# Larger handover and move allowances in the planner of a fused attention and MLP kernel, past the first fifth of the plan

## The chip, the cores and the metric

The kernel runs on one core of one Trainium2 chip. Such a core has five instruction streams: TensorE (PE in the profile; its weight loads are listed apart as PEld), VectorE (DVE), ScalarE (ACT), GpSimd (POOL) and SyncE (SP), which here does nothing but issue DMAs. Every stream runs its instructions strictly in the order in which the program lists them, and waits on semaphores for the others. The metric is the device time of one execution in microseconds (us), as the median of several runs.

## The reference, cut to what matters

```python
# q, k, v: 8 batches x 8 heads x 576 x 64;  f: 8 x 8 x 576
scores = (q @ k.T) / sqrt(64)
cum    = cumsum(log(clip(f, 1e-4, 1)))
scores = where(causal, -1e9, scores + cum[:, None] - cum[None, :])
attn   = exp(scores - max(scores)); attn /= sum(attn) + 1e-9
x      = attn @ v                      # as 4608 tokens x 512
h      = x @ w_in                      # 512 -> 2048
g      = h * tanh(softplus(h))         # Mish
out    = g @ w_out                     # 2048 -> 512
```

## The kernel before

Attention goes by pairs of heads, four pairs a batch, 32 in all. For each pair after the first batch PE multiplies queries by keys (tile `st`) into a PSUM bank `b`; DVE adds the mask and takes the row extreme in one pass (`b<-b,mskw`, and the small `mn`); ACT takes the exponential into one of four buffers (called `rk` or `more_e` by their memory); ACT rounds it to a high fp16 half and DVE subtracts to get the low half (both `hb`); a transposing DMA on the SP queue turns `hb` into `pt`; PE multiplies `pt` by the values `vv`. The sums are normalised (`x<-b,rr`), split into halves (`xp`) and turned by DMA into `xa`, the tokens of the MLP.

The MLP goes by nine chunks of 512 tokens. First layer: `xa` by the weights `wall` into banks b2 and b3, Mish on ACT into `me`, then a high half `gh` (on ACT or DVE) and a low half `gl` (DVE). Second layer: `gh` and `gl` by `wall` into banks b4 to b7, then `ot` and a DMA to memory. Scores use banks b0 to b3 as well while the MLP runs, so b2 and b3 are shared between scores and the first layer. The MLP of one chunk runs while the attention of the next batch is computed; the first 200 us hold the preparation of the weights and the attention of the first batch.

No order is written by hand. `Program` records every operation with its possible engines (`choose` may offer, say, `gh` to ACT or DVE), and `emit` (line 332) lists them in the order that `schedule` (line 370) finds. `schedule` alternates two passes ten times and keeps the best of the orders by its own replay `played` (line 392). `backward` (line 443) walks the plan from its end, with fixed delays from one engine to another (`DELAY`, line 368) and a fixed time for a DMA; the latest start that it finds for an operation becomes its priority. `forward` (line 483) is a list scheduler: it gives each engine the ready operation with the best priority and puts the result ready at its end, plus `DELAY`, plus an allowance from `MARGIN` (line 132), 100 ns for PE, DVE and ACT, 0 for POOL, 300 ns for a DMA. The same sum holds for when a PSUM bank may be used again. `forward` also picks the engine of an operation with several ways (`sooner`, line 506). Planned times are in ns. The order alone reaches the chip: an allowance is no wait in the program, it only makes the planner put other ready work between a producer and its consumer.

Of the kernel before, what the change touches and what calls it, by code (L numbers as in the profile page):

```python
# [129 lines left out]
LOOK = dict(zip(('tensor', 'vector', 'scalar', 'gpsimd', 'sync'), (float(x) for x in ("0", "0", "0", "0", "0",))))  # L130
PRIO = 200
MARGIN = dict(tensor=100,vector=100,scalar=100,gpsimd=0,sync=300)
DRAWS = 4
WORK, LAGS, MOVES = 0.02, 50.0, 300.0
F32COL = 8.3
# [30 lines left out]
class Program:  # L166
# [203 lines left out]
    def schedule(self, deps):  # L370
# [12 lines left out]
        for k in range(FB + 1):  # L383
            end, order, ends = self.forward(deps, succ, [a - b for a, b in zip(rank, self.leads)])
            end = float(np.mean([self.played(succ, order, x) for x in range(DRAWS)])) if DRAWS else end
            if best is None or end < best[0]:
# [56 lines left out]
    def backward(self, deps, succ, order, ends):  # L443

        ops = self.ops
        n = len(ops)
        way = dict(order)
        need = [len(x) for x in succ]
        ready = [0.0] * n
        clock = {q: 0.0 for q in self.NAMES}  # L450
        coming = {q: [] for q in self.NAMES}
        ripe = {q: [] for q in self.NAMES}
        end = max(ends)
        start = [0.0] * n
        for i in range(n):
            if not need[i]:
                heappush(coming[ops[i][0][way[i]][0]], (0.0, i))
        left = n
        while left:
            t, q = min(  # L460
                (clock[q] if ripe[q] else max(clock[q], coming[q][0][0]), q)
                for q in self.NAMES if ripe[q] or coming[q])
            while coming[q] and coming[q][0][0] <= t:
                i = heappop(coming[q])[1]
                heappush(ripe[q], (-ends[i], i))
            i = heappop(ripe[q])[1]
            cost = ops[i][0][way[i]][2]
            clock[q] = t + (max(cost) if q == "sync" else cost[0] / 2.4 + 2.5 if q == "tensor" else cost)
            start[i] = end - clock[q]
            left -= 1  # L470
            for j in deps[i]:
                p, _, c, _ = ops[j][0][way[j]]
                if p == "sync":
                    d = 1580.0 + c[0] + c[1] - max(c)
                else:
                    d = 0.0 if p == "tensor" and q == "tensor" else self.DELAY[p]
                ready[j] = max(ready[j], clock[q] + d)
                need[j] -= 1
                if not need[j]:
                    heappush(coming[p], (ready[j], j))  # L480
        return start

    def forward(self, deps, succ, rank):
# [6 lines left out]
        clock = {q: 0.0 for q in self.NAMES}  # L490
# [11 lines left out]
        def arrive(i):  # L502
            for o, (q, _, _, _) in enumerate(ops[i][0]):
                heappush(coming[q], (ready[i], i, o))
# [22 lines left out]
        while len(order) < n:  # L527
            clock["sync"] = max(clock["sync"], hw, dma - BACK)
            best = None
            for q in self.NAMES:  # L530
                r, c = ripe[q], coming[q]
                while r and taken[r[0][1]]:
                    heappop(r)
                while c and taken[c[0][1]]:
                    heappop(c)
                if r or c:
                    t = clock[q] if r else max(clock[q], c[0][0])
                    if best is None or (t, q) < best:
                        best = (t, q)
            t, q = best  # L540
            while coming[q] and coming[q][0][0] <= t:
                _, i, o = heappop(coming[q])
                if not taken[i]:
                    heappush(ripe[q], (rank[i], i, o))
            skipped, far = [], None
            other = read if q == "tensor" else written
            got = None
            while ripe[q]:
                x = heappop(ripe[q])
                if taken[x[1]]:  # L550
                    continue
                late = max([other.get(b, 0.0) for b in self.banks[x[1]]], default=0.0)
                if late > t:
                    heappush(coming[q], (late, x[1], x[2]))
                    continue
                if len(ops[x[1]][0]) > 1 and sooner(x[1], x[2], q, t):
                    skipped.append(x)
                    continue
                f = self.sets[x[1]]
                if q == "scalar" and f not in (None, table) or q == "tensor" and self.forms[x[1]] != form:  # L560

                    if far is None:
                        far = x
                    else:
                        skipped.append(x)
                    continue
                if far is not None and x[0] > far[0] + (TSWAP if q == "scalar" else 0 if form == (True, True) else MSWAP):
                    heappush(ripe[q], x)
                else:
                    got = x  # L570
                break
            if far is not None:
                if got is None:
                    got = far
                else:
                    skipped.append(far)
            for x in skipped:
                heappush(ripe[q], x)
            if got is None:
                if not ripe[q]:  # L580
                    continue

                later = [clock[p] for p in self.NAMES if p != q and ripe[p]]
                later += [max(clock[p], coming[p][0][0]) for p in self.NAMES if coming[p]]
                clock[q] = max(t + 20.0, min([v for v in later if v > t], default=t + 20.0))
                continue
            key, i, o = got
            wait = [
                (rank[k], k, ok, tk) for tk, k, ok in coming[q]
                if tk <= t + LOOK[q] and rank[k] < key and not taken[k] and len(ops[k][0]) == 1]  # L590
            if wait:
                heappush(ripe[q], got)
                _, i, o, t = min(wait)
            taken[i] = True
            order.append((i, o))
            _, way, cost, lock = ops[i][0][o]
            if way[0][1].startswith("dma_start"):
                hw = max(t, hw) + cost[0]
                clock[q] = t + 50
                dma = max(dma, hw + 650) + cost[1]  # L600
                end, own = dma + 930 + MARGIN["sync"], 0.0
            else:
                if q == "tensor":
                    cols, weight, h = cost
                    slow = 1.0 if left.get(int(t / TICK) - 1, 0.0) >= 3060.0 else 2.0
                    cost = 22.0 if h and half and h != half else cols * slow / 2.4 + (2.5 if slow < 2 else 0.0)
                    a, b = (t + 197.0) / TICK, (t + 197.0 + cols * slow / 2.4) / TICK
                    for k in range(int(a), int(b) + 1):
                        left[k] = left.get(k, 0.0) + weight * (min(b, k + 1) - max(a, k)) / (b - a)
                    half = h  # L610
                    if self.forms[i] != form:
                        form = self.forms[i]
                        cost += MSW * slow
                elif lock:
                    port = max(t, port) + cost
                    cost = port - t
                elif q == "scalar" and self.sets[i] not in (None, table):
                    table = self.sets[i]
                    cost += 1370.0
                clock[q] = t + cost  # L620
                end, own = clock[q], self.DELAY[q] + MARGIN[q]
            ends[i] = end
            for b in self.banks[i]:
                (written if q == "tensor" else read)[b] = end + own
            for j in succ[i]:
                d = 0.0 if q == "tensor" and ops[j][0][0][0] == q else own
                ready[j] = max(ready[j], end + d)
                need[j] -= 1
                if not need[j]:
                    arrive(j)  # L630
# [1594 lines left out]
```

## Time and profile before

| | us |
|---|---|
| median of 3 runs | 1007.24 (1006.58 to 1007.51) |
| the profiled execution | 1006.07 |
| its span, first to last instruction | 1004.3 |
| outside the span | 1.8 |
| busy in the span: PE / DVE / ACT / POOL | 962.7 / 857.5 / 758.1 / 23.0 |

The span is what the trace shows; 1.8 us of the device time lie around it. A share of busy time is a mean over very different stretches, so the stretches have to be read apart. Of PE it also has to be known that a matmul's end is modelled with its pipeline delay, so that a short pause between two matmuls looks shorter in the idle column than it is from start to start.

### The profile page before, as it was taken

What the parts mean: (1) busy time and instruction counts of PE and PEld (TensorE: products, weight loads), DVE (VectorE), ACT (ScalarE), POOL (GpSimd) and SP (SyncE); (2) the same over time, 40 slices, a digit from 0 to 9 for tenths busy, and PEclk for the clock granted to TensorE, in tenths of its full rate; (3) what the DMA queues carried; (4) which work ended last, traced back from release to release, by engine and by line L of the source; (5) the groups of instructions that cost most, each with busy time, mean ns of one, the idle gap of its engine ahead of it and who ended that gap; (6) DMA issues with size and microseconds to landing.
All of it is one profiled execution on the core that took longest, in us unless ns stands there. A gap on an engine that the chain in (4) does not pass through costs nothing.

```text
span 1004.3 us, 22515 instructions
## 1 busy us (share of the span) xinstructions
PE 962.7 (96%) x8384; PEld 598.3 (60%) x8384; DVE 857.5 (85%) x2348; ACT 758.1 (75%) x1492; POOL 23.0 (2%) x79
## 2 busy tenths in 40 slices
PE   6999899999999999999999999899999999999998
PEld 5786455445445565555565555555555566656887
DVE  8899999986779998887888788887798779995895
ACT  3569999986878888888788788788777775654660
POOL 5100000000000000000000000000000000000000
PEclk9799999999999999999999999999999999999999
DMA  7969876598677676677768776777565752000001
GB/s 208 374 213 243 197 168 159 97 200 171 134 138 163 126 147 153 135 177 155 152 138 194 150 151 127 174 136 147 122 131 125 116 86 63 22 1 22 23 1 42
DMA packets 265663, 137.60 MB, mean 137 GB/s; under 512 B 237586, under 2 KB 238802, under 8 KB 265554
## 3 DMA queue, kind: packets, MB, share of 16 engines
q1 hardware_dynamic: 265554, 136.17, 61.5%
q8 instruction: 65, 1.06, 0.4%
q14 instruction: 44, 0.36, 0.1%
HBM read 45.46 MB, written 9.66 MB: 55 GB/s over the span
## 4 chain that ended last, share of the span: by engine, by line
PE 35%; DVE 33%; ACT 16%; DMA 9%; issue 6%; SPq 2%; DVEq 0%; ACTq 0%
PE b L338 35%; DVE b L338 5%; DVE hb L338 4%; DVE me L338 4%; DVE wall L338 3%; DMA pt<-hb 3%; ACT L338 2%; DVE gl L338 2%; DVE hl L338 2%; ACT junk L338 2%; SPq L338 2%; DMA st<-hl 2%; ACT me L338 2%; ACT hb L338 2%; DVE xp L338 2%
## 5 line engine op out<-in xcount | busy, mean ns | idle before, releaser
L338 PEld LDWEIGHTS <-wall 128*128 128x128 f16 x3612 | 345.8, 98 | 280.0 <-issue 23.9
L338 PE MATMUL b<-gh,wall 128*128 128x512 f16 (+1 forms) x1044 | 332.8, 378 | 0.3
L338 PE MATMUL b<-xa,wall 128*128 128x512 f16 (+1 forms) x1590 | 299.4, 331 | 10.2 <-ACT me L338 5.0
L338 PE MATMUL b<-gl,wall 128*128 128x512 f16 (+1 forms) x522 | 197.0, 377 | 0.6 <-DVE gl L338 0.6
L338 DVE SCALAR_TENSOR_TENSOR gl<-me,gsc,gh 128x512 f16<-128x512 f32 x130 | 96.0, 747 | 25.4 <-ACT gh L338 24.5
L338 PE MATMUL b<-st 67*128 67x256 f16 (+11 forms) x672 | 106.2, 298 | 7.4 <-ACT more_e L338 3.3
L338 PEld LDWEIGHTS <-pt 128*128 128x128 f16 (+1 forms) x2424 | 87.8, 101 | 34.1 <-DMA pt<-hb 9.5
L338 PE MATMUL b<-vv,pt 128*128 128x65 f16 (+4 forms) x2464 | 99.7, 197 | 6.3 <-DMA pt<-hb 5.6
L338 DVE CUSTOM_DVE_ANT_0 b<-b,mskw 128x512 f32<-128x512 f32 (+2 forms) x168 | 93.8, 565 | 4.6 <-PE b L338 3.0
L338 DVE TENSOR_TENSOR me<-b,me 128x256 f32<-128x256 f32 x180 | 74.5, 419 | 25.6 <-PE b L338 24.7
L338 ACT ACT_TABLE_LOAD x70 | 89.8, 1283 | 1.9 <-DVE late L338 0.6
L338 PEld LDWEIGHTS <-st 128*128 128x128 f16 (+3 forms) x792 | 60.7, 101 | 50.4 <-issue 13.8
L338 ACT ACTIVATE me<-b,cinv 128x512 f32<-128x512 f32 (+1 forms) x108 | 65.7, 612 | 26.0 <-PE b L338 25.3
L338 ACT ACTIVATE more_e<-b,mn 128x512 f32<-128x512 f32 (+3 forms) x126 | 64.3, 542 | 14.0 <-DVE mn L338 13.3
L338 ACT ACTIVATE rk<-b,mn 128x512 f32<-128x512 f32 (+3 forms) x126 | 64.4, 541 | 12.5 <-DVE mn L338 7.3
L338 DVE TENSOR_TENSOR hb<-rk,hb 128x512 f16<-128x512 f32 x84 | 57.6, 686 | 14.9 <-ACT hb L338 14.8
L338 ACT ACTIVATE me<-me,cinv 128x512 f32<-128x512 f32 x72 | 42.8, 608 | 35.1 <-DVE me L338 34.8
L338 DVE TENSOR_TENSOR hb<-more_e,hb 128x512 f16<-128x512 f32 x84 | 57.6, 686 | 10.4 <-ACT hb L338 10.3
L338 ACT ACTIVATE gh<-me,gsc 128x512 f16<-128x512 f32 x85 | 61.0, 719 | 1.8
L338 ACT ACTIVATE hb<-rk 128x512 f16<-128x512 f32 x84 | 52.8, 628 | 5.4 <-DMA pt<-hb 5.0
L338 ACT ACTIVATE hb<-more_e 128x512 f16<-128x512 f32 x84 | 52.7, 628 | 1.1 <-DMA pt<-hb 0.6
L338 DVE SCALAR_TENSOR_TENSOR hl<-qk,qt,hl 128x576 f16<-128x576 f32 x56 | 44.6, 810 | 2.7 <-ACT hl L338 1.8
(305 smaller groups left out, 1415.7 us busy)
## 6 DMA issues: line engine op xcount, KB each, us to landing
st<-hl SPq DMA_DIRECT2D x168, 144.0 KB
qk<-in_qk_dram SPq DMA_DIRECT2D x30, 576.0 KB
v<-in_v_dram SPq DMA_DIRECT2D x30, 288.0 KB
wall<-in_w_in_dram SPq DMA_DIRECT2D x16, 512.0 KB
wall<-in_w_out_dram SPq DMA_DIRECT2D x16, 512.0 KB
out_dram<-ot SPq DMA_DIRECT2D x32, 256.0 KB
pt<-hb SPq DMA_TRANSPOSE x168
vv<-in_v_dram SPq DMA_DIRECT2D x2, 288.0 KB
```

Of the source, the lines that this page charges most:

```text
L338: r = getattr(real[eng], method)(*a, **kw)
```

## The change

Two constants are new: a planned time of 200,000 ns and a second set of allowances, 300 ns for PE, DVE and ACT, 0 for POOL, 800 ns for a DMA. `forward` takes the second set for operations that it places after 200 us of planned time. `backward` took no allowance at all before; now it adds the second set to every handover whose consumer starts after 200 us (but none from PE to PE). What is computed, and each operation's list of possible engines, stay.

```diff
+LATER = 200000
+MARGIN2 = dict(tensor=300, vector=300, scalar=300, gpsimd=0, sync=800)
@@ backward
+                late = end - clock[q] > LATER
                 if p == "sync":
-                    d = 1580.0 + c[0] + c[1] - max(c)
+                    d = 1580.0 + c[0] + c[1] - max(c) + late * MARGIN2[p]
                 else:
-                    d = 0.0 if p == "tensor" and q == "tensor" else self.DELAY[p]
+                    d = 0.0 if p == "tensor" and q == "tensor" else self.DELAY[p] + late * MARGIN2[p]
@@ forward
-                end, own = dma + 930 + MARGIN["sync"], 0.0
+                end, own = dma + 930 + (MARGIN2 if t > LATER else MARGIN)["sync"], 0.0
@@
-                end, own = clock[q], self.DELAY[q] + MARGIN[q]
+                end, own = clock[q], self.DELAY[q] + (MARGIN2 if t > LATER else MARGIN)[q]
```

The built programs hold the same work in another order. PE keeps its 8028 matmuls of the computation (128x128 filler products on identity tiles go from 148 to 151); SP keeps its 605 DMAs and POOL its list. Where an operation may go to either ACT or DVE the choice moves: ACT has 80 instructions fewer, DVE 36 more.

**Place one, PE and SP at a transposed block of the attention** (644.40 us in the trace of before). PE's rows before; `pt_0` comes from the transposing DMA, `xa1` with `wall` is the first layer of the MLP:

```order
L338 MATMUL b2_0_120<-xa1_90,wall_69 128x512
L338 LDWEIGHTS wall_69
L338 MATMUL b3_0_121<-xa1_90,wall_69 128x512
L338 LDWEIGHTS wall_69
L338 MATMUL b3_0_121<-xa1_90,wall_69 128x512
L338 LDWEIGHTS wall_69
L338 MATMUL b3_0_121<-xa1_90,wall_69 128x512
L338 LDWEIGHTS pt_0_128
L338 MATMUL b1_0_118<-vv_0_113,pt_0_128 128x65
```

PE's rows of the change at the same block:

```order
L340 MATMUL b2_0_120<-xa1_90,wall_69 128x256
L340 LDWEIGHTS wall_69
L340 MATMUL b3_0_121<-qk32_1_109,wall_69 128x256
L340 LDWEIGHTS wall_69
L340 MATMUL b3_0_121<-qk32_1_109,wall_69 128x256
L340 LDWEIGHTS wall_69
L340 MATMUL b3_0_121<-qk32_1_109,wall_69 128x256
L340 LDWEIGHTS wall_69
L340 MATMUL b3_0_121<-ot_1_192,wall_69 128x256
L340 LDWEIGHTS pt_0_128
L340 MATMUL b1_0_118<-vv_0_113,pt_0_128 128x65
```

The block now stands behind more of the MLP: the products that came after it before (the 128x256 ones) stand ahead of it. SP's rows around the DMA that PE waits for, before:

```order
L338 DMA out_0_dram<-ot_0_191 128x512
L338 DMA_TRANSPOSE xa1_90<-xp0_0_143 128x8x128
L338 DMA_TRANSPOSE tv_0_157<-hv_0_156 128x2x128
L338 DMA_TRANSPOSE pt_6_142<-hb_0_152 128x8x128
L338 DMA_TRANSPOSE pt_0_128<-hb_1_153 128x8x128
L338 DMA out_0_dram<-ot_0_191 128x512
```

and now:

```order
L340 DMA st2_0_86<-hl_0_110 64x1152
L340 DMA_TRANSPOSE xa1_90<-xp0_0_143 128x8x128
L340 DMA_TRANSPOSE pt_6_142<-hb_0_152 128x8x128
L340 DMA_TRANSPOSE tv_0_157<-hv_0_156 128x2x128
L340 DMA_TRANSPOSE pt_0_128<-hb_1_153 128x8x128
L340 DMA out_0_dram<-ot_0_191 128x512
```

The transposing DMA of `pt_0` keeps its place behind the same three; an output DMA of 256 KB went from ahead of them to behind.

**Place two, PE at a first-layer product in bank b2** (587.35 us), which the scores held before. Before; `b7<-gl_1` is the second layer, and twelve products into b3 stand above these rows up to the scores:

```order
L338 LDWEIGHTS wall_69
L338 MATMUL b3_0_121<-xa0_89,wall_69 128x512
L338 LDWEIGHTS wall_69
L338 MATMUL b7_0_107<-gl_1_164,wall_69 128x512
L338 LDWEIGHTS wall_69
L338 MATMUL b2_0_120<-xa0_89,wall_69 128x512
```

and now:

```order
L340 MATMUL b4_0_122<-gl_0_161,wall_69 128x512
L340 LDWEIGHTS wall_69
L340 MATMUL b4_0_122<-gh_0_160,wall_69 128x512
L340 LDWEIGHTS wall_69
L340 MATMUL b5_0_123<-gl_0_161,wall_69 128x512
L340 LDWEIGHTS wall_69
L340 MATMUL b2_0_120<-xa0_89,wall_69 128x512
```

The product into b2 now comes after second-layer work, farther from the scores.

**Place three, ACT and DVE at 250 us.** ACT's rows before; `me` is Mish, `x32` the normalised sums of a head:

```order
L338 ACTIVATE hl_0_110<-qk32_0_108,qt_0_150 128x576
L338 ACTIVATE x32_0_140<-b0_0_125,rr_2_147 128x64 x4
L338 ACTIVATE me_2_165<-b2_0_120,cinv3_98 128x512
L338 ACTIVATE gh_2_166<-me_2_165,gsc3_102 128x512
L338 ACTIVATE me_3_171<-b3_0_121,cinv3_98 128x512
L338 ACTIVATE gh_3_172<-me_3_171,gsc3_102 128x512
```

DVE's rows of the change for the same operations:

```order
L340 TENSOR_SCALAR hl_0_110<-qk32_0_108,qt_0_150 128x576
L340 TENSOR_SCALAR gh_2_166<-me_2_165,gsc3_102 128x512
L340 TENSOR_SCALAR hl_0_110<-qk32_0_108,qt_0_150 128x576
L340 SCALAR_TENSOR_TENSOR hl_0_110<-qk32_0_108,qt_0_150,hl_0_110 128x576
L340 TENSOR_SCALAR rr_2_147<-b0_0_125 128x4
```

and, after four more rows of DVE's list:

```order
L340 RECIPROCAL rr_2_147<-rr_2_147 128x4
L340 SCALAR_TENSOR_TENSOR hl_0_110<-qk32_0_108,qt_0_150,hl_0_110 128x576
L340 TENSOR_TENSOR x32_0_140<-b0_0_125,rr_2_147 128x4x64
L340 TENSOR_SCALAR gh_3_172<-me_3_171,gsc3_102 128x512
L340 SCALAR_TENSOR_TENSOR gl_2_167<-me_2_165,gsc3_102,gh_2_166 128x512
```

Both `gh`, the normalisation of four blocks and one rounding `hl` went from ACT to DVE. Over the whole program 22 of the 128x512 `gh`, 14 normalisations (four ACT instructions of 128x64 each, one of 128x4x64 on DVE) and 6 roundings of `vv` go that way, 3 `hl` and 4 of the 128x512 `xp` the other way, and a few smaller ones either way.

## Rows read from the trace of the kernel before

**Rows 1.** The page, part 1: busy time, share of the span, instructions

```profile
PE 962.7 (96%) x8384; PEld 598.3 (60%) x8384; DVE 857.5 (85%) x2348; ACT 758.1 (75%) x1492; POOL 23.0 (2%) x79
```

**Rows 2.** Busy us by stretch; columns: length, PE, PEld, DVE, ACT, POOL, clock, DMA, GB/s

```profile
0.00:50.00 50.00, 38.32 (x477) 30.92 (x477) 42.76 (x105) 23.60 (x56) 18.79 (x51) 0.86 0.85 291
50.00:200.00 150.00, 142.08 (x1292) 85.29 (x1291) 148.75 (x439) 138.53 (x268) 0.99 (x5) 0.99 0.76 180
200.00:300.00 100.00, 95.88 (x760) 49.11 (x759) 73.58 (x211) 77.82 (x161) 0.56 (x4) 1.00 0.78 161
300.00:400.00 100.00, 98.34 (x859) 57.37 (x860) 92.45 (x268) 86.62 (x175) 0.56 (x4) 1.00 0.72 146
400.00:850.00 450.00, 437.51 (x3824) 260.26 (x3822) 372.36 (x1043) 356.43 (x697) 2.08 (x15) 1.00 0.68 138
850.00:1004.30 154.30, 150.53 (x1184) 115.34 (x1181) 127.61 (x287) 75.09 (x138) 0.00 (x0) 1.00 0.06 20
```

**Rows 3.** The same view: the whole stretch in question, and around one drop of the clock

```profile
200.00:850.00 650.00, 631.74 (x5440) 366.74 (x5439) 538.39 (x1521) 520.88 (x1032) 3.20 (x23) 1.00 0.71 143
...
750.00:753.60 3.60, 1.53 (x33) 1.29 (x33) 3.60 (x10) 2.97 (x5) 0.00 (x0) 1.00 0.69 130
753.60:757.00 3.40, 3.40 (x13) 1.64 (x11) 2.94 (x7) 3.36 (x9) 0.00 (x0) 0.50 0.96 219
```

**Rows 4.** Waits of PE after 200 us: total us, times, longest

```profile
PE b L338 <- DMA pt<-hb: 5.0, 6, 1.3
PE b L338 <- ACT me L338: 4.6, 5, 1.9
PE b L338 <- ACT more_e L338: 2.6, 7, 0.8
PE b L338 <- ACT rk L338: 2.0, 6, 0.5
PE b L338 <- ACT evs L338: 1.8, 4, 0.9
PE b L338 <- DVE gl L338: 0.6, 2, 0.4
```

**Rows 5.** Timeline of PE at single waits: start, length, tiles, count, idle before

```profile
328.33 0.82 PE L338 MATMUL b<-xa,wall 128*128 128x256 f16 x6 [1.12 <-ACT me L338]
...
537.72 0.96 PE L338 MATMUL b<-vv,pt 128*128 128x65 f16 x26 [1.10 <-DMA pt<-hb]
...
587.35 1.46 PE L338 MATMUL b<-xa,wall 128*128 128x512 f16 x6 [0.76 <-ACT more_e L338]
...
639.75 3.40 PE L338 MATMUL b<-xa,wall 128*128 128x512 f16 x15 [0.48 <-ACT more_e L338]
644.40 0.99 PE L338 MATMUL b<-vv,pt 128*128 128x65 f16 x27 [1.25 <-DMA pt<-hb]
...
745.40 4.69 PE L338 MATMUL b<-xa,wall 128*128 128x512 f16 x21
...
753.16 1.05 PE L338 MATMUL b<-xa,wall 128*128 128x256 f16 x6 [1.87 <-ACT me L338]
```

**Rows 6.** Groups of instructions by shape: count, busy us, mean ns, idle before

```profile
L338 ACT ACTIVATE gh<-me,gsc 128x512 f16<-128x512 f32 x85 | 61.0, 719 | 1.8
L338 DVE TENSOR_SCALAR gh<-me,gsc 128x512 f16<-128x512 f32 x45 | 21.6, 482 | 14.3 <-ACT me L338 13.7
L338 ACT ACTIVATE x<-b,rr 128x64 f32<-128x64 f32 x68 | 15.8, 315 | 8.6 <-DVE rr L338 8.5
L338 DVE TENSOR_TENSOR x<-b,rr 128x256 f32<-128x256 f32 x39 | 16.3, 419 | 0.7 <-ACT evs L338 0.5
L338 DVE SCALAR_TENSOR_TENSOR vv<-v,cols,vv 128x576 f16<-128x576 f32 x28 | 22.8, 814 | 0.0
L338 DVE TENSOR_SCALAR hl<-qk,qt 128x576 f16<-128x576 f32 x18 | 9.1, 513 | 3.1 <-DMA st<-hl 3.1
L338 DVE CAST xp<-x 128x512 f16<-128x512 f32 x16 | 6.7, 420 | 0.0
```

## The prediction, made before the changed kernel ran

> **What bounds the kernel now.** I read the page first, then busy time by stretch, then PE's waits and its timeline at the single waits. The page gives PE 96%, DVE 85%, ACT 75% [rows 1]; the stretches say that this mixes two regimes [rows 2]. From 50 to 200 us DVE is busy 148.75 of 150 us: that stage lasts as long as DVE's list. From 200 to 850 us PE is busy 631.74 of 650 us [rows 3], DVE 538.39, ACT 520.88: there PE sets the time, and all that can be won is what PE waits. After 850 us PE is busy 150.53 of 154.30 us and the rest is mostly the last output leaving; nothing is to be won there.
>
> How long PE streams is plain from its timeline: 21 matmuls of 512 columns take 4.69 us and 15 take 3.40, so each further one (4.69 - 3.40) / 6 = 0.215 us [rows 5]. The matmuls are the same before and after (three filler products of 128 columns more, 0.2 us in all, in time that PE would wait). So the forecast is a sum over waits of PE.
>
> PE's waits after 200 us are listed by what ended them [rows 4]: transposing DMAs 5.0 us, Mish into `me` on ACT 4.6, exponentials on ACT that free a bank 2.6 + 2.0 + 1.8 = 6.4, and under 1 us each for the rest: some 17 us in all. Each pause is longer from start to start than its idle column says: the run of 15 that begins at 639.75 should let the next matmul begin at 639.75 + 15 x 0.215 = 642.98, it begins at 644.40, 1.42 us later, where the idle column has 1.25 [rows 5]. Added up in that way the transposing DMAs cost 7.2 us, the bank waits behind exponentials about 7, the Mish waits about 5. One thing more hangs on them: from 753.60 to 757.00 the granted clock is 0.50, that is 1.2 GHz instead of 2.4, right after the longest wait of the list (1.87 us at 753.16), with PE busy for 1.53 of the 3.60 us before the drop; 3.40 us at half speed lose 1.7 us [rows 3, 5].
>
> **The change part by part.** It adds no instruction that waits and takes none away. It moves instructions, and a few dozen of them to another engine. What a move is worth I measure by cover: the matmul columns, at 0.215 us per 512, that stand in PE's list between the last matmul on which the waiting one depends through other engines, and the waiting one itself. That is a count in the order, set beside waits in the trace.
>
> *Transposed blocks.* In the order of before 18 blocks have under 9.5 us of cover, and all but a trace of the 7.2 us falls on them (0.4 us each on average); the 105 with more cover lose 0.01 us each on average. In the new order two are left under 9.5 us. The block at 644.40 goes from 7.6 to 11.0 us, the one at 537.72 from 8.8 to 13.1 [rows 5]. Two times 0.4 plus a remainder of 0.4 is 1.2, so the gain is 7.2 - 1.2 = 6.0 us. SP's list around the DMA is nearly the same (place one), so the DMA itself should not start later; that is what this term rests on: were the DMAs later by the 3.4 us that the cover grows at 644.40, nothing would be won there.
>
> *Banks between scores and first layer.* Of 46 such products 28 had under 4 us of cover, and they lose 0.17 to 0.30 us each; 13 are left now. At 587.35 the cover goes from 2.8 to 7.6 us, at 639.75 from 2.4 to 7.8 [rows 5]. At unchanged loss per product 6.4 us become 2.6; I take a gain of 4.0 with what else frees such a bank.
>
> *Mish.* Products that wait for `me` under 1.25 us of cover fall from 23 to 5, but these lost next to nothing. The loss sits in two, at 753.16 and 328.33 (1.87 and 1.12 us idle [rows 5]), both with 1.8 us of cover; now it is 3.9 and 6.6. As these came about by ACT being late, and not by cover alone, I take 3.0 us. The drop of the clock behind the first goes if that wait goes, and can come elsewhere: 1.0 of 1.7 us.
>
> *ACT to DVE.* 22 `gh` at 0.482 us, 14 normalisations at 0.419, 6 `vv` at about 0.814 (the nearest DVE row on `vv`) come to DVE, 3 `hl` at 0.513 and 4 `xp` at 0.420 leave it [rows 6]: 10.6 + 5.9 + 4.9 - 1.5 - 1.7 = 18.2 us more on DVE, nearly all after 200 us. ACT loses 22 x 0.719 + 56 x 0.315 and more, over 30 us. DVE is idle for 650 - 538.39 = 111.6 us between 200 and 850 [rows 3], so most of it finds room: the bounds are 0 and 18.2 us on PE's path, also below 0 as a shorter list on ACT frees banks sooner. In 300 to 400 us DVE is idle for 7.6 us only [rows 2], so some will show. I take a third, 6.0 us, nearer to 0 as PE waits for DVE directly for under 1 us [rows 4].
>
> *The first fifth.* It moves too, since `backward` hands changed priorities down to it. Its length is DVE's list up to the point where PE has enough to do. I counted what DVE must have done ahead of each of PE's matmuls, less the columns ahead of it: the highest such lead rises by 0.7 us. Bounds are -1 and +7: DVE idles 50 - 42.76 = 7.24 us before 50 us [rows 2] and might do so once more. I take 0.7.
>
> Sum: 6.0 + 4.0 + 3.0 + 1.0 = 14.0 won, 6.0 + 0.7 = 6.7 given back, 7.3 us net. The profiled execution of 1006.07 us (span 1004.3 and 1.8 around it) would be 998.8; the median of the runs, 1.17 above it, 1007.24 - 7.3 = 999.9 us.
>
> **The rivals.** *The waits form anew.* Where PE no longer waits for one thing it meets the next one late; of the scores' banks those with under 5 us of cover grow from 28 to 39, and the lists of four engines are new in a thousand places. For it: the waits are many and small, none over 2 us [rows 4]. Against it: the cover grows in nearly every class that lost time, and the classes where it shrinks lost 0.02 us a product. If all 14.0 come back but no more, the time is within 2 us of 1007.2.
>
> *DVE binds.* Its 18.2 us fall where it has no room, at 300 to 400 us, and delay Mish inputs, `gl` and `hb`, on which PE waits. For it: DVE at 92.45 of 100 us there [rows 2]. Against it: 111.6 us of idle time in the stretch [rows 3]. With all of it on the path the time is 1007.2 - 14.0 + 18.2 + 0.7 = 1012.1 us; it is slower than before from the point where more than 13.3 of the 18.2 us, three quarters, reach PE.
>
> The Trainium skill (Perfetto Trace Analysis, section Identifying the Most-Contended Engine) speaks against this change: it calls a matmul busy share a poor measure, wants TensorE judged by its utilisation and by the busy share of weight loads, and calls the engine with the highest occupancy the one to relieve. By that rule DVE (83% from 200 to 850 us, against 56% of PEld [rows 3]) is the limit, work moved to it lengthens the kernel, and the time is 1007.2 + 18.2 = 1025.4 us. The trace does not bear that out: PE's matmuls follow each other at 0.215 us [rows 5] while the weight loads show 56%, so here the loads are hidden and PE is full.
>
> *The first fifth slips.* If DVE's early idle time comes twice, 7 us are lost and the time is about 1007; PE would then show 7 us more of pauses before 200 us.
>
> **How the numbers follow.** A measurement of this kernel tells about 0.2%, 2 us, from no change. The forecast, a net gain of 3 to 13 us (994 to 1004), has 0.66; a larger gain 0.07; a gain between 2 and 3 us 0.03. Waits that form anew, or a slipped first fifth, 0.13 for no change. DVE binding 0.10, 0.02 of them for the rule just named, and 0.01 for other losses. So faster 0.76, same 0.13, slower 0.11. The range from 993.5 to 1007.5 leaves out about 0.07 below and 0.11 above.
>
> **What would show each step.** In the changed kernel's waits of PE after 200 us, the transposing DMAs should fall from 5.0 to about 1 us, the exponentials from 6.4 to under 3, Mish from 4.6 to about 2, and waits on DVE should rise from under 1 us to some 4. PE's busy time should stay near 960 us with a shorter span, DVE's rise to about 875, ACT's fall to about 725. The clock should hold 1.00 from 110 us on. From 50 to 200 us DVE should stay at 99%. The forecast is wrong if PE's waits on DVE eat the gain, if the transposing DMAs land later by as much as their cover grew, or if PE reaches the same matmul at 200 us several us later than before.

## The result, and the profile after

| | us |
|---|---|
| median before, 4 runs | 1007.38 (1006.58 to 1007.97) |
| median after, 4 runs | 994.33 (991.71 to 996.51) |
| ratio | 0.987, 95% interval 0.9845 to 0.9895 |
| the profiled execution after / its span | 991.71 / 989.9 |

The change gains 13.05 us, where the forecast's sum was 7.3. 994.33 us lies inside the range of 993.5 to 1007.5, at its fast end, and the gain at the upper edge of the 3 to 13 us that the forecast called most likely.

The page of the kernel after, part 1 and the TensorE clock in 40 slices (the lines that answer to [rows 1]):

```profile
PE 957.0 (97%) x8387; PEld 597.9 (60%) x8387; DVE 871.0 (88%) x2384; ACT 725.9 (73%) x1412; POOL 20.2 (2%) x79
...
PEclk9999799999999999999999999999999999999999
```

VectorE has 13.5 us more work, ScalarE 32.2 us less, and PE is busy for 5.7 us less. I put that down to short pauses that the modelled ends of the matmuls cover, which counted as busy before. Busy time by stretch, as in [rows 2, 3] (length, then PE, PEld, DVE, ACT, POOL, clock, DMA share, GB/s):

```profile
0.00:50.00 50.00, 37.37 (x480) 30.39 (x482) 43.66 (x107) 24.06 (x57) 16.30 (x51) 0.97 0.85 293
50.00:200.00 150.00, 140.41 (x1277) 84.41 (x1274) 145.94 (x434) 134.62 (x263) 0.70 (x5) 0.97 0.79 181
200.00:300.00 100.00, 99.26 (x807) 51.59 (x806) 86.44 (x246) 76.11 (x144) 0.56 (x4) 1.00 0.82 169
300.00:400.00 100.00, 99.97 (x855) 58.44 (x854) 93.10 (x268) 81.44 (x169) 0.56 (x4) 1.00 0.69 148
400.00:850.00 450.00, 443.44 (x3898) 267.65 (x3896) 391.78 (x1087) 347.69 (x666) 2.08 (x15) 1.00 0.69 138
850.00:989.90 139.90, 136.59 (x1080) 105.41 (x1078) 110.13 (x247) 61.96 (x115) 0.00 (x0) 1.00 0.05 16
200.00:836.00 636.00, 629.62 (x5474) 368.97 (x5473) 557.32 (x1567) 496.64 (x963) 3.20 (x23) 1.00 0.72 146
```

The gain lies after 200 us. The last product of the attention ended at 837.9 us and now ends at 821.1. Leaving out the last 154 us of either kernel, PE is busy 629.62 of 636 us (200 to 836) where it was 631.74 of 650 (200 to 850). PE's waits after 200 us (total, times, longest), against [rows 4]:

```profile
PE b L340 <- DVE gh L340: 2.2, 2, 1.4
PE b L340 <- ACT me L340: 1.5, 2, 0.8
PE b L340 <- ACT xa L340: 0.9, 2, 0.5
PE b L340 <- ACT evs L340: 0.7, 1, 0.7
PE b L340 <- DVE xa L340: 0.6, 1, 0.6
PE b L340 <- DVE me L340: 0.6, 2, 0.4
PE b L340 <- ACT gh L340: 0.4, 1, 0.4
PE b L340 <- DMA pt<-hb: 0.2, 1, 0.2
```

These eight rows hold 7.1 us; the nine of before held 17.4. The waits on the transposing DMAs and on the exponentials (`more_e`, `rk`) are all but gone. New is a wait for `gh` on VectorE.

To compare all kernels I add up, matmul by matmul, the time from one start to the next beyond the matmul's columns at 2.4 GHz. Columns and losses together give the span to within 2 us (904.6 + 101.3 before, 904.8 + 86.0 after). What the columns took longer at half clock is set apart; the rest I call pauses. All 14 kernels have 904.6 to 906.4 us of columns. The loss before 200 us holds, in all of them alike, what products in 32 bits take beyond one pass of their columns: 240 of 65 columns follow each other there at 0.112 us, where 65 columns at 2.4 GHz are 0.027. So in that column only differences tell something. The last three columns are sums of VectorE's own waits after 200 us. All columns but the median are those of one profiled execution of each kernel; that of e8 was the fastest of its 12 (1002.14 us), that of e11 the slowest of its 6 (1016.3).

| kernel | median us | lost before 200 us | lost after 200 us | of it pauses | VectorE's waits: all | for ScalarE | for PE |
|---|---|---|---|---|---|---|---|
| before | 1007.38 | 61.8 | 39.5 | 37.9 | 126 | 77 | 44 |
| after | 994.33 | 63.7 | 22.3 | 21.0 | 96 | 28 | 61 |
| e1_pv_later | 1014.27 | 61.3 | 47.0 | 43.7 | 133 | 79 | 49 |
| e2_change_old_engines | 1006.08 | 70.7 | 28.2 | 28.2 | 116 | 50 | 64 |
| e3_before_new_engines | 1012.95 | 68.3 | 38.0 | 38.0 | 115 | 68 | 43 |
| e4_nudged | 1016.37 | 67.5 | 45.7 | 44.2 | 130 | 84 | 42 |
| e5_forward_only | 1024.10 | 63.0 | 51.6 | 47.8 | 132 | 55 | 69 |
| e6_backward_only | 998.46 | 62.0 | 30.1 | 30.1 | 109 | 48 | 56 |
| e7_from_start | 999.57 | 65.6 | 28.1 | 25.8 | 105 | 33 | 69 |
| e8_change_nudged | 1005.89 | 64.6 | 32.7 | 29.0 | 111 | 32 | 73 |
| e9_forward_nudged | 1025.34 | 59.8 | 60.4 | 53.1 | 141 | 54 | 79 |
| e10_priorities_engines | 1001.67 | 61.9 | 33.6 | 33.6 | 111 | 53 | 48 |
| e11_priorities_moves | 1012.96 | 68.6 | 42.1 | 42.1 | 125 | 78 | 40 |
| e12_double | 1059.69 | 78.2 | 75.7 | 64.8 | 161 | 43 | 106 |

The sum of VectorE's waits says little by itself: its work is nearly the same in all, so a longer span leaves it idle for longer. How that idle time divides between ScalarE and PE is what the experiments turn on.

### The profile page after: what moved, and what is told of

It is laid out like the page before. It is cut to its first block, busy times and chain, and to the rows that moved or that the text cites. A ratio compares the mean times of both kernels' runs of the same rounds, so it can differ in the third digit from the quotient of the medians.

```text
span 989.9 us, 22496 instructions
## 1 busy us (share of the span) xinstructions
PE 957.0 (97%) x8387; PEld 597.9 (60%) x8387; DVE 871.0 (88%) x2384; ACT 725.9 (73%) x1412; POOL 20.2 (2%) x79
## 4 chain that ended last, share of the span: by engine, by line
PE 76%; DVE 14%; DMA 4%; ACT 3%; issue 2%; SPq 1%; DVEq 0%; ACTq 0%
PE b L340 76%; DVE wall L340 3%; DVE b L340 2%; DVE hb L340 1%; DMA st<-hl 1%; DVE gl L340 1%; DMA v<-in_v_dram 1%; SPq L340 1%; DMA pt<-hb 1%; DVE hl L340 1%; ACT L340 1%; DVE x L340 1%; DVE st L340 1%; ACT junk L340 1%; DVE pt L340 1%
## 5 line engine op out<-in xcount | busy, mean ns | idle before, releaser
L340 PE MATMUL b<-gh,wall 128*128 128x512 f16 (+1 forms) x1044 | 327.2, 377 | 2.6 <-DVE gh L340 2.2
L340 PE MATMUL b<-xa,wall 128*128 128x512 f16 (+1 forms) x1590 | 306.5, 334 | 5.5 <-ACT me L340 2.6
L340 PE MATMUL b<-st 67*128 67x512 f16 (+11 forms) x672 | 106.2, 299 | 2.5 <-ACT more_e L340 1.0
L340 ACT ACTIVATE me<-b,cinv 128x512 f32<-128x512 f32 (+1 forms) x108 | 64.5, 613 | 39.6 <-PE b L340 39.1
L340 ACT ACTIVATE rk<-b,mn 128x512 f32<-128x512 f32 (+3 forms) x126 | 64.7, 543 | 10.8 <-DVE mn L340 6.6
L340 ACT ACTIVATE me<-me,cinv 128x512 f32<-128x512 f32 (+1 forms) x72 | 43.0, 609 | 21.8 <-DVE me L340 21.4
L340 ACT ACTIVATE gh<-me,gsc 128x512 f16<-128x512 f32 x63 | 44.7, 716 | 0.8
```

Of the source, the lines that this page charges most:

```text
L340: r = getattr(real[eng], method)(*a, **kw)
```

## The experiments

The median of before was 1007.88 us beside e1 to e4, 1007.12 beside e5 to e8 and 1007.22 beside e9 to e12, of 17 runs each. Unless a diff shows otherwise, the kernel is the change.

**Cover for one class alone.** The order of before, with 19 blocks that had under 9.5 us of cover moved by a program behind later matmuls, until 12 us of columns lie ahead of them:

```diff
+LESS, TO = 9.5, 12.0     # us of columns between a block's maker and its user
-        order = self.warmed(*self.schedule(deps))
+        order = self.spread(self.warmed(*self.schedule(deps)), deps)
```

> The order of before with one thing changed by hand: 19 products of a transposed block with the values, each of which had under 9.5 us of matmul columns in front of it since the last matmul that its data depend on, are put behind later matmuls until they have 12 us. All engines, allowances and the orders of ACT, SP and POOL are those of before; 12 of DVE's 2068 instructions shift with them. If cover is what PE's waits hang on, the 7.2 us of waits on transposing DMAs fall to about 1.2 and the time by about 6 us, to 1001. If the waits only form anew at the next late thing, or if the DMA lands later too, the time stays within 2 us of before. If the gain of the change came from the move of work to DVE or from chance, this shows nothing either.

1014.27 us, ratio 1.0066 (1.0053 to 1.0079). PE's waits after 200 us:

```profile
PE b L343 <- ACT me L343: 10.6, 10, 3.1
PE b L343 <- ACT rk L343: 2.4, 7, 0.5
PE b L343 <- ACT more_e L343: 2.4, 6, 0.8
```

The 5.0 us on transposing DMAs are gone from the list, as the cover says, but the time rose by 6.4 us, which none of the three expectations has. The waits for Mish (`me`) rose from 4.6 to 10.6 us. The wait at 753.16 us [rows 5] grew from 2.03 to 3.23 us, start to start, and two of 1.91 and 1.84 us are new at 541.74 and 649.25 us, soon behind the places where the blocks of 537.72 and 644.40 us stood. As I read it, the products put ahead of the blocks come too early for their own makers.

**Engines and order apart.** e2 takes the change's allowances but binds each of the 1184 operations with a choice to the engine that it had before; e3 takes the old allowances and the engines of the change:

```diff
+WAYS = "..."
+        way = iter(WAYS)
+        self.ops = [x if len(x[0]) == 1 else ([x[0][int(next(way))]], *x[1:]) for x in self.ops]
```

> The change, but every operation that may go to ACT or DVE is bound to the engine that it had before: DVE has its 14.7 us less again, ACT its 25 us more. If cover makes the gain and the engines matter little, it is about 11 us faster than before (996), since fewer blocks are short of cover (3 under 9.5 us, 17 bank products under 4 us, against 18 and 28 before and 2 and 13 in the change). If the moves to DVE cost the 6 us of the prediction, it is faster than the change by about 6 us less the 2 of its thinner cover: 990. If the moves make the gain, it is at 1005 to 1008.

> The order of before, planned with the old allowances, but with every operation bound to the engine that it has in the change: 14.7 us more on DVE, 25 less on ACT. Its cover is that of before (12 blocks under 9.5 us, 27 bank products under 4 us). Cover theory: 1005 to 1008, the same as before. The prediction's give-back: up to 6 us slower, 1013. Moves as the source of the gain: some 994 to 998.

e2: 1006.08 us, ratio 0.9981 (0.9971 to 0.999). After 200 us it loses 28.2 against 39.5 us, so the order without the moves brings 11.3 us there; before 200 us it loses 8.9 us more, and so the time as a whole is what was expected if the moves made the gain. e3: 1012.95 us, ratio 1.0049 (1.0037 to 1.0061), 38.0 us after 200 us and 6.5 more before. VectorE has 19.0 us more work after 200 us (666.0 to 685.0), yet the pauses there are the same (37.9 and 38.0). PE's waits for VectorE do rise, from 1.0 to 5.9 us, while those for ScalarE and DMAs fall by nearly as much. With the new order the kernel that has the moves loses 5.9 us less there than the one that doesn't (22.3 against 28.2). Each is one order against one other, and the next run shows how far two orders can differ for nothing.

**A nudge by 5 ns.** The kernel before with allowances worth the same, in another order:

```diff
-MARGIN = dict(tensor=100,vector=100,scalar=100,gpsimd=0,sync=300)
+MARGIN = dict(tensor=105,vector=105,scalar=105,gpsimd=0,sync=305)
```

> The kernel before with its allowances 5 ns larger everywhere (105 and 305), which reshuffles the order without giving cover (13 blocks under 9.5 us, 27 bank products under 4). Cover theory: within 3 us of before, as the waits that the table of cover gives are the same 28 us. If the gain is the luck of a reshuffled order, it may land anywhere within 13 us of before, on either side.

1016.37 us, ratio 1.0086 (1.0067 to 1.0106): outside the 3 us that cover allowed, and on the slow side. Reordering by itself moves the time by 8.5 us, more than the forecast gain. A single pair of orders can't tell what the allowances do, so from here on orders are read in groups.

**Which pass.** e5 counts more in `forward` alone, e6 in `backward` alone:

```diff
 # e5, backward
-                    d = 0.0 if p == "tensor" and q == "tensor" else self.DELAY[p] + late * MARGIN2[p]
+                    d = 0.0 if p == "tensor" and q == "tensor" else self.DELAY[p]
...
 # e6, forward
-                end, own = clock[q], self.DELAY[q] + (MARGIN2 if t > LATER else MARGIN)[q]
+                end, own = clock[q], self.DELAY[q] + MARGIN[q]
```

> The larger allowances stand only in the pass that places the instructions; the pass that sets the priorities counts the old ones. Theory 1 (time after 200 us goes by how many handovers have too few columns between maker and user): this order has 8 of 123 transposed blocks under 9.5 us of columns (before 18, change 2), 21 of 46 score banks under 4 us (28, 13), 18 of 122 weighted rows under 1.25 us (23, 5). By the prices read off the kernel before that is 19.7 us of late loss against 28.0 before and 14.9 in the change, so some 60% of the late gain of 17 us: late loss 29 us, and with the first 200 us anywhere between 61 and 70 us lost, 997 to 1006 us, middle 1002. Theory 2 (the priorities are what counts): no gain, 1005 to 1012.

> The reverse: the larger allowances stand only in the pass that sets the priorities. Theory 1: 3 of 123 transposed blocks under 9.5 us of columns, but 32 of 46 score banks under 4 us (more than before's 28) and 8 of 120 weighted rows under 1.25 us; by the prices of before 20.7 us of late loss, so late loss about 30 us, and 998 to 1007 us, middle 1003. Waits of TensorE on transposing DMAs after 200 us fall under 1.5 us, those on weighted rows and score banks stay near the 6 us of before. Theory 2 (placement is what counts, priorities bring nothing): 1006 to 1014.

e5: 1024.1 us, ratio 1.0163 (1.015 to 1.0177): slower, where cover promised a gain, and 12 us beyond what theory 2 allowed. e6: 998.46 us, ratio 0.9915 (0.9903 to 0.9928): faster, at the fast edge of what theory 1 said, and against theory 2. VectorE's waits after 200 us (total, times, longest) show what each pass moves. Before:

```profile
DVE hb L338 <- ACT hb L338: 25.1, 30, 2.2
DVE me L338 <- PE b L338: 24.7, 39, 7.2
DVE gl L338 <- ACT gh L338: 24.5, 17, 3.9
DVE gh L338 <- ACT me L338: 13.7, 11, 2.4
DVE ot L338 <- PE b L338: 5.0, 6, 0.8
DVE b L338 <- PE b L338: 4.8, 13, 0.7
```

Placing alone (e5):

```profile
DVE me L340 <- PE b L340: 28.1, 32, 8.6
DVE hb L340 <- ACT hb L340: 23.5, 32, 3.2
DVE b L340 <- PE b L340: 20.4, 25, 2.3
DVE gh L340 <- ACT me L340: 12.2, 15, 1.4
DVE rr L340 <- PE b L340: 10.9, 17, 1.8
DVE gl L340 <- ACT gh L340: 9.9, 11, 2.3
```

Priorities alone (e6):

```profile
DVE me L340 <- PE b L340: 32.9, 35, 5.9
DVE hb L340 <- ACT hb L340: 20.3, 25, 2.7
DVE gl L340 <- ACT gh L340: 7.1, 5, 2.8
DVE b L340 <- PE b L340: 6.7, 12, 1.3
```

Both, the change:

```profile
DVE me L340 <- PE b L340: 31.0, 42, 6.0
DVE gh L340 <- ACT me L340: 12.2, 15, 2.4
DVE b L340 <- PE b L340: 11.3, 19, 1.3
DVE rr L340 <- PE b L340: 8.8, 16, 1.2
DVE hb L340 <- ACT hb L340: 7.6, 20, 0.8
```

Before, VectorE stood still for 24.5 us waiting for `gh` from ScalarE and for 25.1 us waiting for `hb`. Both passes cut the first. Placing alone pays for it: the pass over the scores (`b<-b,mskw`) waits for PE for 20.4 instead of 4.8 us, and the row sums (`rr`) for 10.9. I take it that PE's list now holds other matmuls ahead of those on which VectorE waits; no run shows that by itself. The wait for `hb` is cut in the change (7.6 us) but not in its nudged kernel e8 below (18.2 us).

**The boundary, and the change nudged.**

```diff
 # e7
-LATER = 200000
+LATER = 0
 # e8
-MARGIN2 = dict(tensor=300, vector=300, scalar=300, gpsimd=0, sync=800)
+MARGIN2 = dict(tensor=305, vector=305, scalar=305, gpsimd=0, sync=805)
```

> The change with its boundary taken away: the larger allowances hold from the first instruction on. Theory 1 (the boundary guards the first fifth, where VectorE is the engine that is full): VectorE's list stands ahead of its columns by up to 64.5 us in the first 200 us, against 59.5 before and 60.2 in the change, so the first 200 us lose some 5 us more than the change's 63.7, and the late part stays at the change's 22: 996 to 1000 us. Theory 2 (cover helps there as it does later): the first 200 us lose 58 us or less, 985 to 990 us. Theory 3 (the early loss moves with any reshuffling): anything from 60 to 71 us there, 990 to 1001 us, with no link to the lead.

> The change with its later allowances 5 ns larger (305 and 805 ns), which by itself is worth nothing, but gives another order. The same nudge of the kernel before cost 8.5 us. Theory 1 (the late gain is the cover's, not this order's luck): cover almost as in the change (4 of 121 blocks under 9.5 us, 11 of 46 banks under 4 us, 7 of 122 rows under 1.25 us; 15.5 us against 14.9 by the prices of before), late loss 20 to 28 us; the first 200 us 61 to 71 us; so 989 to 1004 us, and in any case faster than the kernel before. Theory 2 (the change was a lucky draw): late loss 35 us or more, 1004 us or more.

e7: 999.57 us, ratio 0.992 (0.9907 to 0.9933). The first 200 us lose 65.6 us against 63.7 in the change. That is less than the 5 us of theory 1 and no gain as in theory 2; within the 60 to 71 us of most of the other orders, so what the boundary is worth stays open. The 5.2 us that it loses on the change come mostly from after 200 us (28.1 against 22.3). e8: 1005.89 us, ratio 0.9994 (0.997 to 1.0017), the median of 12 runs between 1002.14 and 1014.75. Its late pauses are 29.0 us, of the change's kind and not of before's. But the time is no better than before. Both theories miss: the time lies outside the 989 to 1004 us of theory 1, the late loss of 32.7 us between the two. Against its own counterpart, the nudged kernel before, it is some 10 us faster (1016.37 and 1005.89, measured in different sets), as the change is 13.05 us faster than before.

**Placing alone once more, and the two halves of the priorities.** e9 is e5 with 305 and 805; e10 and e11 are e6 with

```diff
 # e10
+MARGIN2 = dict(tensor=300, vector=300, scalar=300, gpsimd=0, sync=0)
 # e11
+MARGIN2 = dict(tensor=0, vector=0, scalar=0, gpsimd=0, sync=800)
```

> The kernel with larger allowances in the placing pass alone, 5 ns larger still (305 and 805 ns): another order of the same kind. Theory P (what counts is the larger allowance in the pass that sets the priorities): like the five orders without it, 38 to 48 us lost to waits after 200 us, 1006 to 1020 us, no gain on the kernel before. Theory L (the first order of this kind, at 1024.1 us, was an unlucky draw and placement does bring something, as its cover says): 25 to 33 us lost to waits, 995 to 1004 us.

> Only the pass that sets the priorities counts more, and only for handovers from an engine (300 ns); moves by DMA count as before in both passes. Theory E (the handovers from VectorE and ScalarE carry it): 26 to 31 us lost to waits after 200 us as with both, 996 to 1003 us. Theory M (the moves carry it): 38 us or more, 1005 to 1013 us, with the waits on transposing DMAs at 5 us or more. By the cover in columns alone (23.8 us by the prices of before, against 20.7 with both) it would be about 33 us and 1001 us.

> The other half: in the pass that sets the priorities only the moves by DMA count more (800 ns), handovers from an engine as before, placement as before. Theory E: no gain, 38 to 48 us lost to waits after 200 us, 1005 to 1016 us. Theory M: 26 to 31 us, 996 to 1003 us. By the cover in columns (28.0 us by the prices of before, no better than before): no gain, 1005 to 1012 us.

e9: 1025.34 us, ratio 1.0188 (1.0173 to 1.0202), 60.4 us lost after 200 us: slower even than theory P said, and e5 was no unlucky draw. e10: 1001.67 us, ratio 0.9952 (0.9939 to 0.9966), 33.6 us of pauses. e11: 1012.96 us, ratio 1.0062 (1.0044 to 1.008), 42.1 us of pauses. By the times theory E holds: the allowance for a handover from an engine carries the gain, that for a move by DMA brings none by itself. The loss of e10 is a little over the 26 to 31 us of theory E, and is what cover gave (33). e10 keeps 4.9 us of waits on transposing DMAs (before 5.0) and is still faster, so the gain doesn't rest on that row, the largest of before, alone.

**Twice the allowances**, in both passes:

```diff
-MARGIN2 = dict(tensor=300, vector=300, scalar=300, gpsimd=0, sync=800)
+MARGIN2 = dict(tensor=600, vector=600, scalar=600, gpsimd=0, sync=1600)
```

> Both passes as in the change, with twice its later allowances (600 and 1600 ns). Theory 1 (more cover goes on paying): by the prices of before 12.6 us of late loss against 14.9 in the change, so 18 to 22 us lost to waits after 200 us; VectorE's list stands up to 67 us ahead of its columns around 200 us against 60, so the first 200 us and the stretch behind lose 60 to 70 us; 988 to 998 us. Theory 2 (the gain is used up at 300 and 800 ns, and what is left is the draw): 24 to 30 us lost late, 994 to 1004 us.

1059.69 us, ratio 1.0541 (1.0517 to 1.0565): both theories miss by 55 us and more. By the prices of before this order has the best cover of all (3 of 120 blocks under 9.5 us, 8 of 46 banks under 4), and it has the most pauses. PE's waits after 200 us, first two rows, and VectorE's, first two:

```profile
PE b L340 <- DMA pt<-hb: 11.3, 5, 4.4
PE b L340 <- DVE gh L340: 6.1, 8, 1.5
```

```profile
DVE me L340 <- PE b L340: 53.1, 65, 6.6
DVE b L340 <- PE b L340: 28.9, 37, 2.7
```

VectorE waits 106 us for PE (before 44). As I read the two lists, PE then waits for what VectorE made late: five waits on transposing DMAs, up to 4.4 us, though only 3 of 120 blocks are short of cover. No kernel of the twelve beats the change.

**What the groups say.** Pauses after 200 us, by pass:

| larger allowance for engines in | kernels | pauses us | VectorE for ScalarE | VectorE for PE |
|---|---|---|---|---|
| neither pass | before, e1, e3, e4, e11 | 38 to 44 | 68 to 84 | 40 to 49 |
| placing | e5, e9 | 48 to 53 | 54 to 55 | 69 to 79 |
| priorities | e6, e10 | 30 to 34 | 48 to 53 | 48 to 56 |
| both, 300 or 305 ns | after, e2, e7, e8 | 21 to 29 | 28 to 50 | 61 to 73 |
| both, 600 ns | e12 | 65 | 43 | 106 |

No group overlaps another in its pauses, though between priorities alone and both there is only 1.1 us (30.1 and 29.0). That larger allowances of some 300 ns in the priorities make the gain is shown by the runs: each of the six orders that have them is faster than each that doesn't (994.33 to 1006.08 against 1007 to 1025 us). That placing alone costs is shown too, by two orders. What placing adds beside the priorities is not: its pauses are a little shorter, but e6 and e10 without it (998.46 and 1001.67 us) lie among the four that have it. Cover foretold the late loss of e6 and e10 (30 and 33 us, measured 30.1 and 33.6) but not that of e5 (29, measured 51.6) or e12 (18 to 22, measured 75.7). That the gain works through VectorE's waits for ScalarE is read from the table and not shown by a run of its own.

## Why the prediction was right, and where its sum was not

**The bound** held. PE is the engine that is full after 200 us and the gain is a sum over its waits. *Which* waits were counted was right for the change; how the gain hangs on them was not.

**Transposed blocks**, forecast 5.0 to about 1 us in PE's waits, gain 6.0: the row is at 0.2, and the blocks of 537.72 and 644.40 us no longer wait. The step's price was right for this order, but its reason, cover, doesn't carry it: in e1 cover takes the row away and the time rises by 6.4 us all the same, e5 has 8 blocks under 9.5 us instead of 18 and 5.9 us on that row, e8 has 4 and 4.3 us, e12 has 3 and 11.3 us.

**Banks**, exponentials 6.4 to under 3 us, gain 4.0: 0.7 us are left (`evs`). Right, and larger than forecast. (At unchanged loss per product 13 of 28 would leave 3.0 of 6.4 us, not the 2.6 of the prediction.)

**Mish**, 4.6 to about 2, gain 3.0: 1.5 us on ScalarE and 0.6 on VectorE. Right in size. The wait of 328.33 us is gone; that of 753.16 is still there, shorter (start, length, tiles, count, idle before), beside the new one for `gh`:

```profile
642.47 0.81 PE L340 MATMUL b<-gh,wall 128*128 128x512 f16 x3 [0.80 <-DVE gh L340]
...
735.77 0.82 PE L340 MATMUL b<-xa,wall 128*128 128x256 f16 x6 [0.79 <-ACT me L340]
```

**The clock**, gain 1.0, 1.00 from 110 us on: wrong. The drop at 753.6 us went, another came at 837.3, again behind a stretch where PE paused (busy 5.75 of 7.30 us):

```profile
830.00:837.30 7.30, 5.75 (x41) 3.70 (x39) 7.30 (x17) 5.67 (x12) 0.00 (x0) 1.00 0.12 43
837.30:840.70 3.40, 3.03 (x15) 1.99 (x14) 3.40 (x10) 1.11 (x2) 0.00 (x0) 0.50 0.19 67
```

What half clock cost after 200 us went from 1.7 to 1.4 us.

**Sum of the gains**: 14.0 forecast, or 8.0 with the 6.0 given back after 200 us taken off; 17.2 measured (39.5 to 22.3), with it taken off. Start to start, the waits in PE's list went from 14.7 to 4.5 us for ScalarE, from 6.6 to 0.4 for DMAs and from 1.7 to 4.2 for VectorE. The pauses that are too short for the list (up to 0.15 us in the idle column) lost 2.8 us more, and the sum had nothing for them. So of the 9.2 us by which it was short, 3.5 stand in what VectorE gave back, 3.2 in ScalarE's waits and 2.8 in short pauses; the clock gave 0.7 less than forecast.

**ACT to DVE**, 6.0 given back: the term that was off most. The work came as counted (VectorE's busy time after 200 us from 666.0 to 681.4 us, 15.4 of the 18.2), and PE's waits for VectorE rose from 1.0 to 3.4 us, near the 4 forecast. But no third of it reached the end: 2.5 us start to start. The step took VectorE's idle time as room that is partly in the wrong place; most of it after 200 us was VectorE itself waiting, 77 of 126 us for ScalarE, and that fell to 28. The moves alone don't do that. With the new engines and the old allowances (e3) the 24.5 us that VectorE waits behind `gh` fall to 6.0, but a `gh` made on VectorE waits there for `me` from ScalarE instead, 26.8 us where it was 13.7:

```profile
DVE gh L341 <- ACT me L341: 26.8, 22, 2.5
DVE gl L341 <- ACT gh L341: 6.0, 7, 3.3
```

With the old engines and the new allowances (e2) the two are 13.7 and 3.1 us, in the change 12.2 and 2.4. So it is the new order that takes these waits away, and in e3 the moves cost nothing in sum while PE waits less for ScalarE and DMAs. The bound of 0 that the step named was nearer than its 6.0.

**The first fifth**, 0.7 given back, bounds -1 and +7: 1.9 measured (61.8 to 63.7). From 50 to 200 us VectorE did not stay at 99% but fell to 97% (145.94 of 150 us), and the granted clock from 0.99 to 0.97; before 50 us the clock rose from 0.86 to 0.97. The lead of VectorE's list, from which 0.7 was taken, doesn't tell these orders apart: by my count of the orders, which no row here shows, it is 59 to 60 us in the change and in e2 (57 to 60 in e3 and e4), and these lose 63.7, 70.7, 68.3 and 67.5 us. Only e7 and e12, where it is well above (64.5 and 67 us), lose more than the change as it would have it (65.6 and 78.2). The clock tells more: in these 200 us it stands at 0.50 for 17.1 us before, 13.7 in the change, 20.5 in e2 and 27.3 in e3, e4 and e11. What the columns took longer by it I estimate, from the clock records and the columns of the matmuls, at 5.5, 5.4, 7.8, 11.4, 10.8 and 10.3 us. That is nearly all by which e3 and e4 lose more than before there (5.9 of 6.5 and 5.3 of 5.7 us), but only 2.3 of the 8.9 us of e2. What else sets these 200 us, and why one order falls to half clock for longer, stays open.

So 14.0 - 6.0 - 0.7 became 17.2 - 1.9 = 15.3 us of lost time (14.4 in the spans, 13.05 by the medians). Part of it is this order's luck. The four orders with both passes at 300 or 305 ns lie at 994.33, 999.57, 1005.89 and 1006.08 us, and the change is the fastest of them; the 999.9 us of the forecast is nearer to their middle (1002.7) than to the change. The kernel before is the fastest of its own five orders, too, whose middle is 1012.96 us; from middle to middle it is some 10 us.

**The rivals.** *The waits form anew* did not happen in the change, but its mechanism is real: in e1, e5, e9 and e12 the waits rise in spite of more cover, and e4 shows what a new order is worth without any purpose (8.5 us). The prediction gave it too little; that the gain held owes much to the priorities pass, of which the prediction said only that it moves the first fifth. *DVE binds*: no, VectorE is busy 557.32 of 636 us, 88%, and PE 629.62. The rule of the Trainium skill (Perfetto Trace Analysis, Identifying the Most-Contended Engine), as the prediction applied it, gave 1025.4 us. As to the weight loads the trace disagrees, since with them at 58% (368.97 of 636) and VectorE 15.4 us fuller the kernel is 13 us faster. But that section names the utilisation of TensorE beside them, and the prediction mentions it without working it out. Worked out from the rows and columns of the matmuls in the trace, at 2.4 GHz, it is 90% from 200 to 850 us before, above VectorE's 83%, and by it TensorE is the engine to relieve. *The first fifth slips*: not here. Its price (7 us; by the prediction's own terms that would be 1006.2 us, not 1007) was paid in e2, e3 and e4 (8.9, 6.5 and 5.7 us), but in e3 and e4 nearly all of it at half clock and not as a second idle time of VectorE.

## What to carry to other kernels

Where in-order engines follow a planned list, ask what a planner's allowance does to the priorities before asking how far it sets producer and consumer apart: here the first gained, and the second alone lost. Twice as much in both cost 5%, so the size has to be tried. Judge such a change by groups of orders, each nudged by something worth nothing, since one order against another can differ by 8 to 12 us for no reason that a reader of the code could name. And before costing work that moves to another engine, read what that engine is waiting for in its idle time. Work moved off ScalarE shifted VectorE's wait to the step before it as long as the order stayed the old one (e3); with the new order the wait went away.

## What the runs showed that was not expected

The granted clock of one and the same program is not the same from run to run. The 12 runs of e8 have mean clocks from 0.973 to 0.990 and spans from 1012.9 down to 1000.3 us, the longest spans at the lowest clocks. The stretches at 1.2 GHz can be long: in e3 the clock is at 0.50 for 23.9 us while PE is busy throughout, after 10.2 us in which PE was busy for 8.11 (first two lines e3, third the same stretch of before):

```profile
75.00:85.20 10.20, 8.11 (x100) 6.61 (x100) 10.20 (x25) 5.34 (x14) 0.14 (x1) 1.00 0.80 208
85.20:109.10 23.90, 23.90 (x137) 18.76 (x136) 18.74 (x64) 18.64 (x42) 0.14 (x1) 0.50 0.88 229
```

```profile
85.20:109.10 23.90, 20.03 (x125) 12.00 (x124) 23.61 (x80) 23.16 (x51) 0.14 (x1) 0.93 1.08 246
```

VectorE and ScalarE, busy 23.61 and 23.16 us there before, are busy 18.74 and 18.64 us in e3: VectorE waits for PE there for 4.4 us (2.5 for `rr`, 1.9 for `b`), and for none before. In the stretch that VectorE's list sets, a slow PE makes VectorE wait in its turn.
